# Strassen's scheme for the gate and value products of a fused attention, experts and gated layer, with their weights narrowed ahead of time and kept in DRAM

## The chip, the cores and the metric

The kernel runs on one core of a Trainium2 chip. The metric is the device time of one execution in microseconds; it is compared by the median of several runs. A profile of one execution comes with it: the "span" is the time from its first to its last instruction, and the execution's own time is a little longer.

The engines are named as in the profile: PE (TensorE, matmuls), PEld (its weight loads), DVE (VectorE), ACT (ScalarE), POOL (GpSimd) and SP (SyncE, which issues the DMAs). SBUF is the working memory of 128 partitions, PSUM the memory into which PE writes its sums.

## The reference

Three layers are computed in a row, in float32 and close to its precision:

```python
# attention: q, k, v are [2, 8, 1152, 64]; q is averaged over pairs of rows
q_pool = q.reshape(B, H, S // 2, 2, D).mean(axis=3)
attn = softmax(q_pool @ k.T / sqrt(D));  x = attn @ v      # x: 1152 tokens (2 batches x 576) x 512
# four experts, all of them for every token, weighted by p
for e in range(4):
    out += p[:, e:e+1] * (np.maximum(x @ w1[e], 0) @ w2[e])   # w1 [4,512,1024], w2 [4,1024,512]
# gated layer: w_gate, w_val [512,1536] and w_out [1536,512] come as float64
g = x @ w_gate
return (g * sigmoid(g) * (x @ w_val)) @ w_out                 # [1152, 512]
```

## The kernel before

Every matrix product is made from float32 split in two: a high half `hi` in the reduced format fp32r and the rest `lo = x - hi`. A product is then three matmuls, hi*hi, hi*lo and lo*hi (`gemm`, L918). ACT makes the high half with a copy, DVE (or POOL) the low half with a subtraction.

The token dimension has two batches of 576 tokens. Attention of the first batch runs alone; attention of the second runs together with the first batch's experts; then the second batch's experts run alone on PE; then the gated layer follows for all 1152 tokens. Nothing before the second batch's experts is touched by the change.

*Experts.* Each expert has 8 hidden groups (512 inputs, 128 outputs) and 4 output groups. A weight "piece" is 128 partitions x 512 elements; it is loaded by SP into one of three buffers `wraw`, split by `split_hi` (L350, ACT) and `split_lo` (L357, DVE) into `whi` and `wlo` (two buffers each), and used by 24 matmuls of 288 columns (`products`). A group's sums lie in a pair of PSUM banks, `p0` or `p1` in turn (`expert_bank`); `evict_h` and `evict_h2` (L974, L978) take a hidden group out, `evict_y` (L994, DVE) and `add_y` (L1000, POOL) an output group, into `yacc`.

*Gated layer* (`gated`, L1119). The results `yacc` of both batches are split into `yhi` and `ylo` (L1131, L1132). For each of 12 column chunks, first the gate's and then the value's weights are loaded as 64-bit words (`w64`), narrowed to float32 on DVE (`narrow`, L320: five instructions on L326, L329, L331 and L333), split, and multiplied with the tokens in three stretches of 384: 12 matmuls each, 864 in all. ACT and DVE make silu (L1160, L1161), DVE multiplies by the value (L1167), ACT and POOL split the product for the next layer (L1168, L1169). The output products follow, 324 matmuls of 512 columns: five token tiles together for each weight tile, then the others one by one.

*What sets the order.* `Plan` takes every step with a due time, a cost and what it reads, writes and holds; `arrange` orders the steps by a list schedule over them, and each engine executes its instructions strictly in that order. Attention and the first batch's experts are ordered so; the second batch's experts are only sorted by due time, and `gated` stands in the order in which it is written. Both of these are outside the planner's manual schedule: there the framework's own scheduler may still move instructions.

## Time and profile before

| | |
|---|---|
| median of 3 runs | 912.93 us (912.82 to 914.72) |
| the profiled execution | 913.23 us, of which the span is 911.5 us |
| PE, share of the span | 97% |
| DVE, ACT, POOL | 65%, 51%, 43% |
| DMA | 72.31 MB, mean 79 GB/s |

PE works nearly all the time, so the other shares matter only where they hold PE up. A matmul's duration in the trace is longer than the distance between two matmul starts, since they overlap; the distance is what a matmul costs. The stages that the change touches are the last three: the second batch's experts, the gate and value products, and the output products. The rows further down give their edges.

### The profile page before, as it was taken

What the parts mean: (1) busy time and instruction counts of PE and PEld (TensorE: products, weight loads), DVE (VectorE), ACT (ScalarE), POOL (GpSimd) and SP (SyncE); (2) the same over time, 40 slices, a digit from 0 to 9 for tenths busy, and PEclk for the clock granted to TensorE, in tenths of its full rate; (3) what the DMA queues carried; (4) which work ended last, traced back from release to release, by engine and by line L of the source; (5) the groups of instructions that cost most, each with busy time, mean ns of one, the idle gap of its engine ahead of it and who ended that gap; (6) DMA issues with size and microseconds to landing.
All of it is one profiled execution on the core that took longest, in us unless ns stands there. A gap on an engine that the chain in (4) does not pass through costs nothing.

```text
span 911.5 us, 14995 instructions
## 1 busy us (share of the span) xinstructions
PE 886.3 (97%) x5916; PEld 843.7 (93%) x5916; DVE 590.0 (65%) x895; ACT 463.9 (51%) x790; POOL 388.3 (43%) x266
## 2 busy tenths in 40 slices
PE   6998999999999999999999999999999999999998
PEld 5777778889999999999999999999999999999886
DVE  5778888797666576766855334333478988888700
ACT  5878777877776667766653232232322333333110
POOL 3476555866676885785570000202023333222000
PEclk9999999999999999999999999999999999999999
DMA  5022112313322331212125332323233222323210
GB/s 142 23 68 74 42 52 63 89 62 86 92 66 62 96 104 52 61 55 64 47 72 162 92 95 82 94 81 101 83 97 104 93 87 76 93 90 96 70 70 35
DMA packets 122102, 72.31 MB, mean 79 GB/s; under 512 B 32304, under 2 KB 117296, under 8 KB 122032
## 3 DMA queue, kind: packets, MB, share of 16 engines
q1 hardware_dynamic: 122032, 71.36, 26.8%
q8 instruction: 46, 0.75, 0.3%
q14 instruction: 24, 0.20, 0.1%
HBM read 68.96 MB, written 2.38 MB: 78 GB/s over the span
## 4 chain that ended last, share of the span: by engine, by line
PE 87%; DVE 6%; ACT 3%; issue 2%; POOL 1%; DMA 0%; SPq 0%; DVEq 0%; POOLq 0%; ACTq 0%
PE ps L918 41%; PE g L918 16%; PE av L645 12%; PE o L918 8%; PE sc L538 4%; PE sc L539 3%; DVE acc L567 1%; ACT s L556 1%; PE mt L573 1%; PE tr L482 1%; DVE wlo L357 1%; PE tr L508 1%; ACT kt L498 1%; PE m L595 1%; DVE kt L500 1%
## 5 line engine op out<-in xcount | busy, mean ns | idle before, releaser
L612 POOL TENSOR_TENSOR s<-s,m 128x864 f32<-128x864 f32 x64 | 132.1, 2084 | 71.2 <-ACT m L605 67.9
L350 ACT ACTIVATE whi<-wraw 128x512 fp32r<-128x512 f32 x128 | 80.5, 629 | 155.4 <-PE ps L918 149.4
L918 PE MATMUL ps<-xhi,whi 128*128 128x288 f32 x512 | 152.5, 298 | 1.3 <-DVE hlo L978 1.3
L918 PE MATMUL ps<-hhi,whi 128*128 128x288 f32 x512 | 152.3, 297 | 0.0
L918 PE MATMUL ps<-hhi,wlo 128*128 128x288 f32 x512 | 151.1, 295 | 0.0
L918 PE MATMUL ps<-xhi,wlo 128*128 128x288 f32 x512 | 151.0, 295 | 0.0
L918 PE MATMUL ps<-xlo,whi 128*128 128x288 f32 x512 | 151.0, 295 | 0.0
L918 PE MATMUL ps<-hlo,whi 128*128 128x288 f32 x512 | 150.9, 295 | 0.0
L357 DVE TENSOR_TENSOR wlo<-wraw,whi 128x512 fp32r<-128x512 f32 x96 | 84.6, 881 | 92.3 <-ACT whi L350 92.3
L1000 POOL TENSOR_TENSOR yacc<-yacc,yt 128x576 f32<-128x576 f32 x24 | 42.5, 1770 | 189.2 <-DVE yt L994 189.2
L556 ACT ACTIVATE s<-sc 128x576 f32<-128x576 f32 (+1 forms) x160 | 94.3, 601 | 47.8 <-PE sc L539 46.2
L918 PEld LDWEIGHTS ps<-xhi,whi 128*128 128x128 f32 x512 | 96.2, 188 | 1.7 <-issue 1.5
L918 PE MATMUL g<-yhi,wlo 128*128 128x384 f32 x288 | 96.4, 335 | 0.5 <-DVE wlo L357 0.5
L918 PE MATMUL g<-yhi,whi 128*128 128x384 f32 x288 | 96.2, 335 | 0.5 <-ACT yhi L1131 0.5
L918 PEld LDWEIGHTS ps<-xlo,whi 128*128 128x128 f32 x512 | 96.3, 188 | 0.0
L918 PE MATMUL g<-ylo,whi 128*128 128x384 f32 x288 | 96.3, 334 | 0.0
L918 PEld LDWEIGHTS ps<-hlo,whi 128*128 128x128 f32 x512 | 96.3, 188 | 0.0
L918 PEld LDWEIGHTS ps<-hhi,whi 128*128 128x128 f32 x512 | 96.2, 188 | 0.0
L918 PEld LDWEIGHTS ps<-hhi,wlo 128*128 128x128 f32 x512 | 96.2, 188 | 0.0
L918 PEld LDWEIGHTS ps<-xhi,wlo 128*128 128x128 f32 x512 | 96.2, 188 | 0.0
L538 PE MATMUL sc<-qhi,kt 128*128 128x288 f32 x288 | 90.5, 329 | 5.5 <-DVE acc L567 3.6
L618 ACT ACTIVATE s<-s 128x864 f32<-128x864 f32 x96 | 87.9, 921 | 6.1 <-DVE s L612 4.4
(97 smaller groups left out, 1965.9 us busy)
## 6 DMA issues: line engine op xcount, KB each, us to landing
wraw<-in_moe_w_dram SPq DMA_DIRECT2D x128, 256.0 KB, 2.7
w<-in_moe_w_gate_dram SPq DMA_DIRECT2D x12, 512.0 KB, 3.6
w<-in_moe_w_val_dram SPq DMA_DIRECT2D x12, 512.0 KB, 3.6
w<-in_moe_w_out_dram SPq DMA_DIRECT2D x12, 512.0 KB, 3.5
qraw<-in_q_dram SPq DMA_DIRECT2D x32, 144.0 KB, 2.3
kraw<-in_k_dram SPq DMA_DIRECT2D x14, 288.0 KB, 4.0
v<-in_v_dram SPq DMA_DIRECT2D x8, 288.0 KB, 4.0
vraw<-in_v_dram SPq DMA_DIRECT2D x8, 288.0 KB, 3.0
```

What stands on the lines that cost most here:

```text
L350: nc.scalar.activation(out=hi, in_=t, func=AF.Copy)
L357: eng.tensor_tensor(out=lo, in0=t, in1=hi.bitcast(F32), op=ALU.subtract)
L482: nc.tensor.matmul(pt[:, m * P : (m + 1) * P], kr[:, c].rearrange("p h d -> p (h d)"), ident, is_transpose=True,)
L498: nc.scalar.activation(out=kt[me, sl], in_=pt[me, : 3 * P], func=AF.Copy)
L538: nc.tensor.matmul(ps, wt, qhi, start=True, stop=False)
L539: nc.tensor.matmul(ps, wt, qlo, start=False, stop=True)
L556: nc.scalar.activation(out=s[:, c : c + n, :], in_=ps[:, :n, :W], func=AF.Copy)
L612: eng.tensor_tensor(out=sg, in0=sg, in1=m.unsqueeze(1).to_broadcast([P, 3, W]), op=ALU.subtract)
L618: nc.scalar.activation(out=sg, in_=sg, func=AF.Exp)
L645: nc.tensor.matmul(avs[u][:, :W], w[:, c].rearrange("p t d -> p (t d)"), e, start=(c == 0 and n == 0), stop=(c == KC - 1 and n == len(term ...
L918: nc.tensor.matmul(ps, w, x, start=first and n == 0, stop=last and n == len(terms) - 1)
L1000: nc.gpsimd.tensor_tensor(out=y, in0=y, in1=yts[o], op=ALU.add)
```

## The change

*Products.* Strassen's scheme (Winograd's form) is applied to the gate and value products. Tokens are halved by batch, the 512 inputs into two halves of 256, and the weights' columns into two chunks of 128. A group `n` is two chunks of the gate (n even) or of the value weights (n odd), 12 groups in all. Instead of eight block products a group has seven (`PRODUCTS`, `ORDER`), each of 12 matmuls of 288 columns into a pair of PSUM banks (`product`), 84 products named P0 to P83. Their token operands are blocks of `yacc` or sums of them: `B11`, `B21`, `B22`, and `T1` to `T4`, made in place (`sum_tokens`) and split (`operand_hi`, `operand_lo`).

*Sums.* The four quarters of a group's result come from the seven sums: ACT copies four of them out (`copy_sum`), DVE adds (`add_sum`, four a group, each with one input in PSUM), POOL adds (`add_temp`, three a group). Then ACT's tanh, and DVE's `gate` or `value` in place in SBUF.

*Weights.* All 24 tiles of gate and value weights and 8 of 12 of the output weights are loaded and narrowed during the second batch's experts (`due_wide`: ACT makes the upper part, DVE clamps, shifts and joins). POOL makes the scheme's sums of the weight blocks (`sum_weights`, four a group). SP writes blocks and sums of a group to DRAM (`store_weights`, 512 KB and 384 KB) and reads them back when the products need them (`load_weights`); they are split only then.

*Order.* The second batch's experts and the whole gated layer now go through one `Plan` with `arrange`. The second batch's experts use four bank pairs in turn instead of two. The output products take eight token tiles together for each weight tile, and the ninth at the end; the split of the gated results (`hidden_hi`, `hidden_lo`) moves there, and that of the last token tile is made apart (`end_hi`, `end_lo`).

The tables that set the order: `NARROW`, `OPERAND_DUE`, `SUM_DUE` and others hold due times of these steps; `STEPS` and `BANKS` set the order of the first 21 products and their banks by hand.

```diff
+LATER_SPLIT = (-1.55, -1.29)
+NARROW = (2.48, 10.9, -7.66)
+NARROW_DUE = (0.68, 0.1, 0.2, 4.7, 0.4)
+WEIGHT_DUE = (14.1, 10.6, 10.7, 10.8, 11.5, 11.6)
...
+OUT_FIRST = 8
...
         self.room = room
-        self.psum = ("sc", "av", "m")
-        self.shared = ("v", "vh", "vl")
+        self.psum = ("sc", "av", "m", "G")
+
+        self.shared = ("v", "vh", "vl", "ready")
...
-    def narrow(i, words):
-
-        _, a, b = words.shape
-        words = words.rearrange("p a b -> p (a b)").bitcast(I32)
...
         def expert_bank(group):
-            return "p1" if len(group) == 3 else f"p{(group[0] * (FC1 + MC) + group[1]) % 2}"
+            if len(group) == 3:
+                return "p1"
+            return f"p{(group[0] * (FC1 + MC) + group[1]) % (4 if b else 2)}"
...
+    def load_wide(j):
+        if j < NPIECE:
+            src = columns((wg, wv)[j // 2 % 2], 0, MC, j // 4 * 2 + j % 2)
+        else:
+            c = j - NPIECE
+            src = wo[c * P : (c + 1) * P, :].unsqueeze(1)
+        wides[j] = pools["late"].tile([P, *src.shape[1:]], I64, tag="w64", name=f"w64_{j}", bufs=2)
+        nc.sync.dma_start(out=wides[j], in_=src)
...
+    def take_high(j):
+
+        ups[j] = pools["late"].tile(list(wides[j].shape), F32, tag="up", name=f"up{j}", bufs=1)
+        nc.scalar.activation(out=ups[j], in_=words(j, 1).bitcast(F32), func=AF.Copy, scale=DOWN)
+
+    def clamp(j):
+        nc.vector.tensor_scalar(ups[j], ups[j], LIMIT, -LIMIT, op0=ALU.min, op1=ALU.max)
...
+    def take_low(j):
...
+            n = j // 2
+            bits[n] = pools["st"].tile([P, 2, MC, P], I32, tag="wk", name=f"wk{n}", bufs=3)
+        nc.vector.tensor_scalar(narrowed(j), words(j, 0), 29, None, op0=ALU.logical_shift_right)
+
+    def join(j, m):
+        amount, op = ((3, ALU.logical_shift_left), (SIGN, ALU.bitwise_and))[m]
+        out = narrowed(j)
+        nc.vector.scalar_tensor_tensor(
+            out=out, in0=ups[j].bitcast(I32), scalar=amount, in1=out, op0=op, op1=ALU.bitwise_or
+        )
+
...
+    def sum_weights(n, m):
+
+        if m == 0:
+            wsums[n] = pools["st"].tile([P, 3, 2, P], F32, tag="ws", name=f"ws{n}", bufs=2)
+        s2, s3, s4 = (wsums[n][:, x] for x in range(3))
+        a11, a12, a21, a22 = (weights(n, r, k) for r in range(2) for k in range(2))
+        out, a, b, op = (
+            (s3, a11, a21, ALU.subtract),
+            (a21, a21, a22, ALU.add),
+            (s2, a21, a11, ALU.subtract),
+            (s4, a12, s2, ALU.subtract),
+        )[m]
+        nc.gpsimd.tensor_tensor(out=out, in0=a, in1=b, op=op)
...
+    def store_weights(n, m):
+        if m:
+            nc.sync.dma_start(out=wd[n, :, 4:7], in_=wsums[n])
+        else:
+            nc.sync.dma_start(
+                out=wd[n, :, 0:4].rearrange("p (a k) b c -> p a (k b) c", a=2),
+                in_=bits[n].bitcast(F32),
+            )
+
...
+    PRODUCTS = {
+        1: (0, "B11"), 2: (1, "B21"), 5: (2, "T1"), 4: (3, "T4"),
+        6: (4, "T2"), 7: (5, "T3"), 3: (6, "B22"),
+    }
+    ORDER = (1, 2, 5, 6, 7, 3, 4)
+    STEPS = [(n, p) for n in range(NP) for p in ORDER]
+    STEPS[:21] = (
+        [(n, p) for n in range(2) for p in ORDER[:3]] + [(2, 1), (2, 2), (0, 6), (0, 7), (0, 3)]
+        + [(1, 6), (1, 7), (0, 4), (1, 3), (1, 4)] + [(2, p) for p in ORDER[2:]]
+    )
...
+    def weight_hi(n, g):
+        if g < 3:
+            t = pools["gw"].tile([P, 2, 2, 2, P], F32R, tag="wq", name=f"wq{n}_{g}", bufs=7)
+        else:
+            t = wp.tile([P, 1, 2, 2, P], F32R, tag=single_home(n), name=f"wq{n}_{g}", bufs=2)
+        wsplits[n, g] = t
+        nc.scalar.activation(out=t[:, :, 0], in_=weight_part(n, g), func=AF.Copy)
+
+    def weight_lo(n, g):
+        t = wsplits[n, g]
+        nc.vector.tensor_tensor(
+            out=t[:, :, 1], in0=weight_part(n, g), in1=t[:, :, 0].bitcast(F32), op=ALU.subtract
+        )
+
+    SOURCE = {
+        "B11": (0, 0), "B21": (0, 2), "B22": (1, 2),
+        "T1": (0, 0), "T2": (0, 0), "T3": (1, 0), "T4": (0, 2),
+    }
+    TERMS = {
+        "T1": ((1, 0), (0, 0)), "T2": ((1, 2), (0, 0)),
+        "T3": ((1, 2), (1, 0)), "T4": ((0, 2), (0, 0)),
+    }
...
+    def sum_tokens(name, c):
+        (b0, o0), (b1, o1) = TERMS[name]
+        nc.vector.tensor_tensor(
+            out=source(name, c), in0=yaccs[b0][:, o0 + c, :], in1=yaccs[b1][:, o1 + c, :],
+            op=ALU.subtract,
+        )
...
+    BANKS = (0, 1, 2, 0, 1, 3, 0, 1, 0, 1, 2, 0, 1, 2, 3, 0, 1, 2, 3, 0, 1)
...
+    def product(i, s):
+        if i not in sums:
+            sums[i] = pair(sum_bank(i), f"P{i}")
+        quarter = PRODUCTS[STEPS[i][1]][0]
+        w = wsplits[STEPS[i][0], quarter // 2][:, quarter % 2]
+        t = operands[PRODUCTS[STEPS[i][1]][1]]
+        gemm(
+            sums[i][:, s, :W],
+            [
+                (w[:, x, c], t[:, y, c, subs[s]])
+                for c in range(2)
+                for x, y in ((0, 0), (0, 1), (1, 0))
+            ],
+        )
...
+    def copy_sum(n, i, to):
+        nc.scalar.activation(out=place(n, to), in_=sums[i][:, :, :W], func=AF.Copy)
+
+    def add_sum(n, i, to, other):
+        nc.vector.tensor_tensor(
+            out=place(n, to), in0=sums[i][:, :, :W], in1=place(n, other), op=ALU.add
+        )
+
+    def add_temp(n, to, other):
+        t = place(n, to)
+        nc.gpsimd.tensor_tensor(out=t, in0=t, in1=place(n, other), op=ALU.add)
...
+    def gate(n, q):
+        t = place(n, q)
+        nc.vector.scalar_tensor_tensor(
+            out=t, in0=tanhs.pop((n, q)), scalar=1.0, in1=t, op0=ALU.add, op1=ALU.mult
+        )
...
+        def due_wide(j, t):
+            d = NARROW_DUE
+            at(
+                t + NARROW[2] if j < NPIECE + OUT_FIRST else t - 9, "SP", 0.6, load_wide, j,
+                writes=[("w64", j)], takes=[("w64", ("w64", j))],
+            )
...
+            at(
+                t + d[2], "DVE", 0.7, take_low, j,
+                reads=[("w64", j)] + ([] if opens else [("bits", j - 1)]),
+                writes=[("bits", j)],
+                takes=[("ok" if first else "wraw" if c >= 0 else "wk", tile[0])] if opens else [],
+                uses=[] if opens else tile,
+            )
+            for m in range(2):
+                at(
+                    t + d[3 + m], "DVE", 0.7, join, j, m, kind="port",
+                    reads=[("up", j)], writes=[("bits", j)], uses=tile,
...
+        for i, (n, p) in enumerate(STEPS):
+            t = t0 + i * SLOT
+            if p == ORDER[0]:
+                due_split_weights(n, t0 + 7 * SLOT * n if n > 2 else t0)
+            quarter, name = PRODUCTS[p]
+            g = quarter // 2
+            for s in range(2):
+                at(
+                    t + s * SLOT / 2, "PE", 6 * PITCH, product, i, s, kind="r",
+                    reads=[("wh", n, g), ("wl", n, g)] + [(x, name, c) for x in ("rh", "rl") for c in range(2)],
+                    writes=[("P", i, s)] + ([] if s else [("P", i, 1)]),
+                    takes=[] if s else [(sum_bank(i), ("PT", i))],
+                    uses=[("QS", n, g), ("PT", i)] + [("OP", name)] * (name in ("B11", "B21")),
+                )
+            t += SLOT
+            d = SUM_DUE
+            if p == 1:
+                due_copy(n, i, "s1", t + d[0])
+            elif p == 2:
+                due_copy(n, i, 0, t + d[1])
+                due_temp(n, 0, "s1", t + d[2])
+                due_result(n, 0, t)
+            elif p == 6:
+                due_add(n, i, "u2", "s1", t + d[3])
+                due_add(n, place_of[n, 5], "u4", "u2", t + d[4])
+            elif p == 7:
+                due_add(n, i, "u3", "u2", t + d[5])
+                due_add(n, i, 3, "u4", t + d[6])
+                due_result(n, 3, t)
+            elif p == 3:
+                due_copy(n, i, 1, t + d[8])
+                due_temp(n, 1, "u4", t + d[9])
+                due_result(n, 1, t)
+            elif p == 4:
+                due_copy(n, i, 2, t + d[10])
+                due_temp(n, 2, "u3", t + d[11])
+                due_result(n, 2, t)
```

PE, at the end of the second batch's experts. Before, the last rows of `ps` are followed by the gate's first sum:

```order
L918 MATMUL ps_7686<-hlo_7489,whi127_7705 128x288
L918 MATMUL ps_7686<-hhi_7487,wlo127_7706 128x288
L918 MATMUL g_7793<-yhi_7773,whi128_7742 128x384
L918 MATMUL g_7793<-ylo_7774,whi128_7742 128x384
L918 MATMUL g_7793<-yhi_7773,wlo128_7743 128x384
L918 MATMUL g_7793<-yhi_7773,whi128_7742 128x384
```

Now twelve-matmul products follow (`wqN_g` are the split weights of group N, part g):

```order
L884 MATMUL ps_8103<-hlo_7908,whi127_8112 128x288
L884 MATMUL ps_8103<-hhi_7899,wlo127_8113 128x288
L884 MATMUL P0_8173<-opB11_5636,wq0_0_7982 128x288 x12
L884 MATMUL P1_8189<-opB21_5652,wq0_0_7982 128x288 x12
L884 MATMUL P2_8214<-opT1_8048,wq0_1_7995 128x288 x12
L884 MATMUL P3_8235<-opB11_5636,wq1_0_7936 128x288 x12
L884 MATMUL P4_8253<-opB21_5652,wq1_0_7936 128x288 x12
L884 MATMUL P5_8273<-opT1_8048,wq1_1_7990 128x288 x12
L884 MATMUL P6_8292<-opB11_5636,wq2_0_8145 128x288 x12
L884 MATMUL P7_8311<-opB21_5652,wq2_0_8145 128x288 x12
L884 MATMUL P8_8327<-opT2_8154,wq0_2_8067 128x288 x12
L884 MATMUL P9_8343<-opT3_8271,wq0_2_8067 128x288 x12
```

The first eight products need B11, B21 and T1 alone, of groups 0, 1 and 2; T2 is first used by P8 and T3 by P9.

DVE, in the hidden groups of one of the second batch's experts. Before, weight halves and evictions alternate:

```order
L357 TENSOR_TENSOR wlo98_6729<-wraw98_6639,whi98_6728 128x512
L978 SCALAR_TENSOR_TENSOR hlo_6704<-ps_6674,hhi_6702 128x576
L357 TENSOR_TENSOR wlo99_6766<-wraw99_6672,whi99_6765 128x512
L978 SCALAR_TENSOR_TENSOR hlo_6741<-ps_6709,hhi_6737 128x576
L357 TENSOR_TENSOR wlo100_6801<-wraw100_6707,whi100_6800 128x512
L978 SCALAR_TENSOR_TENSOR hlo_6776<-ps_6746,hhi_6774 128x576
L357 TENSOR_TENSOR wlo101_6836<-wraw101_6744,whi101_6835 128x512
L978 SCALAR_TENSOR_TENSOR hlo_6811<-ps_6781,hhi_6809 128x576
```

Now the narrowing of wide tiles 10 and 11 (`up`, `wk5`) stands between them:

```order
L942 SCALAR_TENSOR_TENSOR hlo_6337<-ps_6272,hhi_6326 128x576
L1115 TENSOR_SCALAR up10_6332<-up10_6332 128x512
L1130 TENSOR_SCALAR wk5_6357<-w64_10_6276 128x512
L1135 SCALAR_TENSOR_TENSOR wk5_6357<-up10_6332,wk5_6357 128x512
L338 TENSOR_TENSOR wlo83_6363<-wraw83_6260,whi83_6362 128x512
L942 SCALAR_TENSOR_TENSOR hlo_6384<-ps_6309,hhi_6372 128x576
L1135 SCALAR_TENSOR_TENSOR wk5_6357<-up10_6332,wk5_6357 128x512
L1130 TENSOR_SCALAR wk5_6357<-w64_11_6321 128x512
L338 TENSOR_TENSOR wlo84_6401<-wraw84_6300,whi84_6400 128x512
L942 SCALAR_TENSOR_TENSOR hlo_6424<-ps_6353,hhi_6411 128x576
L1115 TENSOR_SCALAR up11_6419<-up11_6419 128x512
L1135 SCALAR_TENSOR_TENSOR wk5_6357<-up11_6419,wk5_6357 128x512 x2
```

Between two weight halves two or three narrowing instructions stand, some of which wait for ACT's `up` or for the wide load.

DVE, in the middle of the gate stage. Before, a stretch of the loop over column chunks (`bits` and `up` are the narrowing, `th` and `g` the results):

```order
L357 TENSOR_TENSOR wlo137_8322<-bits137_8317,whi137_8321 128x512
L331 TENSOR_SCALAR bits140_8505<-w64_140_8325 128x512
L333 SCALAR_TENSOR_TENSOR bits140_8505<-up140_8502,bits140_8505 128x512
L1161 SCALAR_TENSOR_TENSOR th_8327<-th_8327,g_8301 128x384
L333 SCALAR_TENSOR_TENSOR bits140_8505<-up140_8502,bits140_8505 128x512
L326 TENSOR_SCALAR up141_8568<-w64_141_8386 128x512
L329 TENSOR_SCALAR up141_8568<-up141_8568 128x512
L1161 SCALAR_TENSOR_TENSOR th_8343<-th_8343,g_8330 128x384
L357 TENSOR_TENSOR wlo138_8383<-bits138_8378,whi138_8382 128x512
L1161 SCALAR_TENSOR_TENSOR th_8359<-th_8359,g_8346 128x384
```

Now one group's sums, with the next group's weight halves (`wq7`) and the gates among them (`s1`, `u4` are the temporaries, `sil3` the gate's results):

```order
L1303 TENSOR_TENSOR s1_6_8968<-P45_9014,s1_6_8968 128x576
L1208 TENSOR_TENSOR wq7_0_9047<-wr7_0_8995,wq7_0_9047 128x2x256
L1208 TENSOR_TENSOR wq7_1_9056<-wr7_0_8995,wq7_1_9056 128x2x256
L1303 TENSOR_TENSOR u4_6_9077<-P44_8997,s1_6_8968 128x576
L1303 TENSOR_TENSOR s1_6_8968<-P46_9030,s1_6_8968 128x576
L1303 TENSOR_TENSOR sil3_9005<-P46_9030,u4_6_9077 128x576
L1208 TENSOR_TENSOR wq7_2_9066<-wr7_1_9021,wq7_2_9066 128x2x256
L1208 TENSOR_TENSOR wq7_3_9085<-wr7_1_9021,wq7_3_9085 128x256
L1317 SCALAR_TENSOR_TENSOR sil3_9005<-th6_3_9106,sil3_9005 128x576
L1317 SCALAR_TENSOR_TENSOR sil3_9005<-th6_1_9115,sil3_9005 128x576
L1317 SCALAR_TENSOR_TENSOR sil3_9005<-th6_2_9155,sil3_9005 128x576
L1324 TENSOR_TENSOR g6_9136<-g6_9136,sil3_9005 128x576
```

The narrowing has gone from this stage, and sums of PSUM with a temporary have come; `s1_6` is the operand of POOL's additions as well.

## Rows read from the trace of the kernel before

**Rows 1.** The page's parts 1 and 2: share and instructions, then tenths by slice.

```profile
span 911.5 us, 14995 instructions
...
PE 886.3 (97%) x5916; PEld 843.7 (93%) x5916; DVE 590.0 (65%) x895; ACT 463.9 (51%) x790; POOL 388.3 (43%) x266
...
PEclk9999999999999999999999999999999999999999
```

**Rows 2.** The chain that ended last: start us, us, engine, what.

```profile
472.98 197.18 PE ps L918 x1488
...
685.44 3.35 POOL yacc L1000
...
834.23 73.49 PE o L918 x324
```

**Rows 3.** PE's timeline at the stage edges: start us, us, engine, what.

```profile
479.18 0.29 PE L918 MATMUL ps<-xhi,whi 128*128 128x288 f32 x1
...
682.70 0.33 PE L918 MATMUL g<-yhi,whi 128*128 128x384 f32 x1
...
834.07 0.39 PE L918 MATMUL o<-whi,gh 128*128 128x512 f32 x1
...
907.33 0.39 PE L918 MATMUL o<-oh,gl 128*128 128x512 f32 x1
```

**Rows 4.** Stretches: us, busy PE, PEld, DVE, ACT, POOL, clock, DMA share, GB/s.

```profile
479.20:682.70 203.50, 203.50 (x1539) 203.50 (x1537) 88.34 (x130) 60.08 (x100) 21.46 (x12) 1.00 0.33 98
...
691.00:834.20 143.20, 143.20 (x828) 143.20 (x827) 122.96 (x215) 48.22 (x94) 43.22 (x35) 1.00 0.28 89
```

**Rows 5.** DVE's timeline in the gate stage.

```profile
690.21 0.69 DVE L333 SCALAR_TENSOR_TENSOR bits<-up,bits 128x512 int32<-128x512 int32 x1
...
690.81 0.55 DVE L1161 SCALAR_TENSOR_TENSOR th<-th,g 128x384 f32<-128x384 f32 x1
...
692.20 1.42 DVE L333 SCALAR_TENSOR_TENSOR bits<-up,bits 128x512 int32<-128x512 int32 x2
...
694.11 0.43 DVE L329 TENSOR_SCALAR up<-up 128x512 f32<-128x512 f32 x1
...
696.45 0.42 DVE L331 TENSOR_SCALAR bits<-w 128x512 int32<-128x512 int32 x1
...
697.52 0.55 DVE L1167 TENSOR_TENSOR g<-th,g 128x384 f32<-128x384 f32 x1
...
697.98 1.04 DVE L333 SCALAR_TENSOR_TENSOR bits<-up,bits 128x512 int32<-128x512 int32 x1
```

**Rows 6.** Groups in the second batch's experts: total us, mean ns, idle before.

```profile
L357 DVE TENSOR_TENSOR wlo<-wraw,whi 128x512 fp32r<-128x512 f32 x63 | 43.4, 689 | 85.4 <-ACT whi L350 85.4
...
L978 DVE SCALAR_TENSOR_TENSOR hlo<-ps,hhi 128x576 fp32r<-128x576 f32 x32 | 24.0, 751 | 0.0
...
L1132 DVE TENSOR_TENSOR ylo<-yacc,yhi 128x576 fp32r<-128x576 f32 x4 | 3.0, 755 | 2.0 <-ACT yhi L1131 2.0
...
L350 ACT ACTIVATE whi<-wraw 128x512 fp32r<-128x512 f32 x63 | 39.7, 631 | 133.4 <-PE ps L918 133.4
```

**Rows 7.** POOL's timeline, in three stretches.

```profile
466.15 1.30 POOL L357 TENSOR_TENSOR wlo<-wraw,whi 128x512 fp32r<-128x512 f32 x1
...
473.29 1.44 POOL L1000 TENSOR_TENSOR yacc<-yacc,yt 128x576 f32<-128x576 f32 x1
...
697.23 1.25 POOL L1169 TENSOR_TENSOR gl<-g,gh 128x384 fp32r<-128x384 f32 x1 [8.44 <-ACT gh L1168]
...
710.22 1.01 POOL L1169 TENSOR_TENSOR gl<-g,gh 128x384 fp32r<-128x384 f32 x1 [0.23 <-ACT gh L1168]
```

**Rows 8.** Two dense stretches, and the weight loads' issues (KB, us to landing).

```profile
5.00:10.00 5.00, 3.19 (x15) 2.93 (x16) 1.57 (x3) 2.30 (x5) 0.44 (x1) 1.00 0.90 215
...
478.00:483.00 5.00, 5.00 (x40) 5.00 (x39) 4.97 (x7) 1.31 (x3) 1.81 (x1) 1.00 0.96 294
...
wraw<-in_moe_w_dram SPq DMA_DIRECT2D x128, 256.0 KB, 2.7
```

More of the change, by code (lines that the diff above doesn't have):

```diff
@@ L920, in gemm @@
             )
-    def three(n, whi, wlo, xhi, xlo):
-        return [
-            (a(c), x(c)) for c in range(n) for a, x in ((whi, xhi), (whi, xlo), (wlo, xhi))
-        ]
     yaccs = {}
@@ L1095, in experts @@
                     if e:
+                        last = b and e == NE - 1 and o >= MC // 2
                         at(
-                            due(n - 1) + 0.7, "POOL", 1.45, add_y, o, kind="port",
+                            due(n - 1) + 0.7, "DVE" if last else "POOL", 0.76 if last else 1.45,
+                            add_y, o, nc.vector if last else nc.gpsimd, kind="port",
                             reads=[y], writes=[("y", b, o)],
@@ new lines, in tile_kernel @@
+    pools = {}
+    wides, ups, bits, wsums, wraws, wsplits, operands = ({} for _ in range(7))
+    sums, temps, sils, tanhs, gs, ghs, wos, ends, outs, ots = ({} for _ in range(10))
+    NPIECE = 2 * FC2
+    NP = FC2
+    TT = NT // P
+    wd = dram.tile([NP, P, 7, 2, P], F32, tag="wd", name="wd")
+    od = dram.tile([OUT_FIRST, P, DM], F32, tag="od", name="od")
+    def load_wide(j):
[6 more added lines that the diff above has]
+        nc.sync.dma_start(out=wides[j], in_=src)
@@ new lines, in gate, with value, hidden_home, hidden_hi @@
+    def gate(n, q):
[3 more added lines that the diff above has]
+        )
+    def value(n, q):
+        t = place(n, q)
+        eng = nc.gpsimd if n == NP - 1 else nc.vector
+        eng.tensor_tensor(out=t, in0=t, in1=place(n - 1, q), op=ALU.mult)
+    def hidden_home(c):
+        return ("acc", "B11", "B21", "acc")[c % 4]
+    def hidden_hi(c):
+        tag = hidden_home(c)
+        pool = acc if tag == "acc" else pools["bz"]
+        ghs[c] = pool.tile([P, 2, NT], F32R, tag=tag, name=f"gh{c}")
+        nc.scalar.activation(out=ghs[c][:, 0], in_=gs[c], func=AF.Copy)
@@ new lines, in out_bank, with out_sum, out_product @@
+    def out_bank(t):
+        return f"p{t // 2 % 4}"
+    def out_sum(t):
+        if t // 2 not in outs:
+            outs[t // 2] = pair(out_bank(t), f"out{t // 2}")
+        return outs[t // 2][:, t % 2]
+    def out_product(c, t):
+        hi, lo = wos[c]
+        if t < TT - 1:
+            gh, gl = (ghs[c][:, x, t * P : (t + 1) * P] for x in range(2))
+        else:
+            gh, gl = (ends[0][:, c, x] for x in range(2))
+        gemm(out_sum(t), [(gh, hi), (gh, lo), (gl, hi)], c == 0, c == FC2 - 1)
```

561 lines of the change are left out of this document (405 added, 156 removed).

## The prediction, made before the result was known

> **What bounds the kernel now.** I read the page's busy shares first, then the chain that ended last, then PE's timeline at the stage edges, and the other engines last. TensorE (PE) is busy 97% of the span at the upper of its two clocks, 2.4 GHz: 9 tenths or more were granted in every slice [rows 1]. The chain ends in three blocks of matmuls with one detour between the first two: 1488 expert matmuls without a gap, a hop over a 3.35 us GpSimd (POOL) addition, the gate and value products, the output products [rows 2]. So time is what PE has to do from the second batch's experts on, and little else. The edges give the price of each stage [rows 3]. The second batch's experts run from 479.18 to 682.70: 203.52 us for 1536 matmuls of 288 columns, 0.1325 us each. The gate and value products run to 834.07: 151.37 us for 864 matmuls of 384 columns, handover included. The output products: 323 steps to 907.33, 0.2268 us each.
> Beside PE the experts leave room: in 203.5 us VectorE (DVE) is busy 88, ACT 60, POOL 21. In the gate stage DVE is busy 123 of 143.2 [rows 4]. The change moves work from the second place to the first.
>
> **The change part by part.**
> *Products.* 864 matmuls go (151.37 us). In their place stand 12 groups of 7 products of 12 matmuls, 1008 of 288 columns, the experts' shape and kind: 1008 x 0.1325 = 133.56 us. That is 17.81 us less. Seven eighths of 151.37 would be 132.4: the shorter matmul pays more per column and gives 1.1 us back.
> *Output and end.* The same 324 matmuls, 324 x 0.2268 = 73.48 us, in another order (eight token tiles for each weight tile, the ninth at the end). From the last matmul's end (907.33 + 0.23) to the span's end 3.94 us remain for a copy and a store [rows 1, 3]; I keep them.
> *Sum.* Attention, the first batch and the second batch's expert matmuls keep their order, so 682.70 stands: 682.70 + 133.56 + 73.48 + 3.94 = 893.68 us of span. The profiled execution took 913.23 us for its span of 911.5, so 1.73 us lie around it: 895.4 us if PE never waits. (Its own time stands 0.3 us above the median of 912.93.) What follows is what PE may wait for.
> *Narrowing beside the experts.* 32 tiles of 128x512 (24 of gate and value weights, 8 of output weights) are narrowed there: on DVE a clamp and a shift of 0.43 and 0.42 and two joins that take 1.42 together [rows 5], 2.27 us a tile, 73 us in all; on ACT one copy each, at 0.63 like the weight copy [rows 6], 20 us. DVE had 63 weight halves of 0.689, 32 evictions of 0.751 and 16 more of a like size [rows 6]: 79.5 us. With four halves of B11 and B21 (0.755) the sum is 156 of 203.5 us, and ACT 80. POOL gains 48 sums of 128x256, which the trace does not show: 384 elements take 1.01 and 512 take 1.30 [rows 7], so about 0.7, with 0 and 1.30 as ends; 34 us, and ten additions to yacc of 1.44 [rows 7]. PE waits if a weight half is late. A piece lasts 24 x 0.1325 = 3.18 us; its successor's buffer comes free as it starts, ACT takes 0.63 and DVE 0.69, so 1.8 us of slack stand against a DVE queue that now always has a join or a shift in front (0.7, or 1.04 when POOL holds it up [rows 5]). Four accumulator pairs instead of two let an eviction end two groups, 6.4 us, later than before. I take 1.0 us of waiting; the ends are 0 and 12 (the rival below).
> *The weights' way through DRAM.* In the experts' 203.5 us the queue moves 61 x 256 KB (expert weights), 32 x 512 (wide weights), 12 x 896 out, 8 x 256 out, 4 x 288 and 1920 KB back: 49.0 MB, 241 GB/s, where the trace has 98 [rows 4]. The densest stretches ran 294 GB/s at a busy share of 0.96, and 215 at 0.90 with the small rows of q and k [rows 8]: 167 to 205 us of transfer. At the first the transfers fit with a fifth to spare, and I take that, since these are rows of 512 B and more. A weight load lands in 2.7 us alone [rows 8]; with a wide load and a store of 512 and 384 KB ahead, 1408 KB / 294 = 4.9 us more, it lands in 7.6, and three buffers give it 9.5. SP issues in order, so a store that waits for POOL holds the next weight load too; the 1.9 us that remain are its cover.
> *The handover.* The old stage's own wait for the last expert columns is in the 151.37 and goes with it. Late next: T2 and T3 need the last expert columns. The new order puts eight products (B11, B21, T1 of three groups) ahead of T2, 8 x 1.59 = 12.7 us, and T3 is read 14.3 us in. DVE has 14 instructions of 0.755 to do by then (two columns of experts, the token sums, their halves), 10.6 us, with two POOL additions of 1.44 in between: 13.5 against 14.3. The cover is thin for the first 21 products; I take 1.2 us, between 0 and 4.
> *Evictions in the gate stage.* Per group (11.13 us of PE): DVE four sums from PSUM (0.751), four gates or values (0.755, by ylo, two inputs in SBUF and 576 elements [rows 6]), 3.5 weight halves (0.689), 8.5 us; ACT four copies, two tanh on average, 3.5 halves, 9.5 instructions at about 0.63, 6.0; POOL three additions of 1.44 [rows 7], 4.3. Each engine fits alone. A sum bank is wanted again four products later, 3.2 us after the sums that read it can start; 0.4 us of waiting over the rest, 0 to 3. So 895.4 + 1.0 + 1.2 + 0.4 = 898.0 us.
>
> **The port, weighed.** DVE's instructions with both inputs in SBUF stretch when POOL works: a join of 0.69 took 1.04 beside POOL's 1.25 at 697.23, while a product with one input in PSUM took its usual 0.55 there [rows 5, 7]. The two do not run side by side, then. The Trainium skill (SBUF — State Buffer, Who interferes with whom) says it as a rule: a DVE instruction with two SBUF inputs and a GpSimd one that reads SBUF exclude each other, and the loser waits for the whole instruction. The trace agrees: 0.35 us more for that join. The rule speaks against this change, which gives POOL more to do beside a fuller DVE; what it would make of the time is rival (3).
>
> **Rivals.**
> (1) No wait at all: 895.4. For it: PE had no gap in 203 us of experts. Against: DVE's spare time was 115 us there and is 48 now.
> (2) The experts starve. Each of the 12 weight sets brings two stores and two wide loads; if each costs PE 1 us, by a late weight half or load, 12 us: 898.0 + 11 = 909. For: 241 of 294 GB/s, one in-order queue. Against: 9.5 us of buffers, four banks.
> (3) The port decides the gate stage, and the change loses. Of each group's 11.13 us DVE has 2.6 spare; POOL wants 4.3. If all of it stops DVE, a group takes 12.8, 12 x 1.67 = 20.0 us: 895.4 + 20.0 + 1.0 = 916.4, slower than before. It costs from 2.6 us of blocking a group on, and cancels the gain at 4.1 of 4.3. Against: four of the twelve DVE instructions read PSUM and are not held, and a DVE instruction starts 0.09 us before the one ahead of it ends (690.21 + 0.69 against 690.81 [rows 5]), 1.0 us more spare a group.
>
> **How the numbers follow.** The forecast, 898.0 with 896 to 902 of its own, gets 0.62; rival (1) 0.13; rival (2), spread over 902 to 912, 0.19; rival (3) 0.06. A change under 0.2% (1.8 us, 911.1 to 914.8) cannot be told from none here: 0.02 of (2) falls there. Faster 0.92, same 0.02, slower 0.06. The range, 894.5 to 908.0, takes in (1) and most of (2), and leaves out (3) and the end of (2).
>
> **What would show it.** PE's 1008 products spaced 0.1325 us; the first one at about 682.7 to 684; idle of PE before expert matmuls under 2 us in total, with wlo or hlo as the releaser; the handover's waits on T2, T3 or on sums, none over 2 us; DVE busy near 160 of the experts' 203 us; transfers at a busy share of 0.7 to 0.85 there. The prediction is wrong if expert matmuls wait for weight loads or wlo again and again, if DVE is busy all through the gate stage with its two-input instructions stretched beside POOL, or if the clock falls below 2.4 GHz after such waits.

## The result, and the profile after

The changed kernel takes 898.5 us (median of 4 runs, 897.19 to 901.6) against 912.88 for the kernel before in the same comparison: a ratio of 0.9843, 95% interval 0.9815 to 0.9872, or 14.4 us less. The forecast was 898.0. The profiled execution took 898.72 us, and its parts are what the rest of this text compares.

The page of the changed kernel, busy time and granted clock:

```profile
span 896.9 us, 15607 instructions
PE 872.0 (97%) x6060; PEld 827.7 (92%) x6060; DVE 672.7 (75%) x943; ACT 522.0 (58%) x880; POOL 445.3 (50%) x316
PEclk9999999999999999999999999999999999999999
```

PE has 97% as before [rows 1], and a shorter span: it still bounds the kernel. The chain that ended last, from the second batch's experts on (start us, us, engine, what):

```profile
472.77 90.99 PE ps L884 x686
...
563.78 1.86 DVE wlo L338
565.68 6.38 PE ps L884 x46
572.44 6.63 PE ps L884 x48
579.08 104.94 PE ps L884 x790
684.02 14.39 PE P L884 x108
698.50 0.77 DVE s L1303
699.29 0.77 DVE u L1303
700.11 118.41 PE P L884 x888
818.52 74.57 PE out L884 x324
```

Before, this stretch was three blocks with one detour at the handover [rows 2]. Now the expert block is cut three times (565.68, 572.44, 579.08), the products once (700.11), and the outputs not at all. The hop over POOL's addition at the handover is gone. PE's timeline gives the edges that answer to [rows 3]:

```profile
478.97 0.29 PE L884 MATMUL ps<-xhi,whi 128*128 128x288 f32 x1
...
683.86 0.29 PE L884 MATMUL P<-opB,wq 128*128 128x288 f32 x1
...
818.36 0.40 PE L884 MATMUL out<-ohi,gh 128*128 128x512 f32 x1
...
892.69 0.39 PE L884 MATMUL out<-ohi,end 128*128 128x512 f32 x1
```

The three stages took 204.89, 134.50 and 74.33 us (the last from first to last matmul start); before they took 203.52, 151.37 and 73.25. The products alone give 16.87 us; experts and outputs give 2.45 back.

The stretches of the experts and of the products (busy PE, PEld, DVE, ACT, POOL, then clock, DMA share, GB/s):

```profile
479.20:684.00 204.80, 204.38 (x1538) 203.56 (x1537) 172.57 (x258) 84.49 (x142) 61.59 (x59) 1.00 0.75 239
...
702.00:818.50 116.50, 116.50 (x877) 116.50 (x877) 103.79 (x130) 60.26 (x103) 51.55 (x33) 1.00 0.26 81
```

Against [rows 4] DVE's work in the experts has doubled (88 to 172.6 us) and the traffic has gone from 98 to 239 GB/s; PE lost 1.37 us by it.

The first of the three cuts, in the timeline of ACT, POOL, DVE and PE:

```profile
559.11 0.67 ACT L1112 ACTIVATE up<-w 128x512 f32<-128x512 f32 x1 [2.58 <-DMA w<-in_moe_w_val_dram]
...
562.54 0.69 ACT L1112 ACTIVATE up<-w 128x512 f32<-128x512 f32 x1 [2.24 <-DVE wk L1135]
...
563.12 0.62 ACT L332 ACTIVATE whi<-wraw 128x512 fp32r<-128x512 f32 x1
563.66 1.43 POOL L964 TENSOR_TENSOR yacc<-yacc,yt 128x576 f32<-128x576 f32 x1 [4.55 <-DVE yt L958]
...
563.78 1.85 DVE L338 TENSOR_TENSOR wlo<-wraw,whi 128x512 fp32r<-128x512 f32 x1 [0.27 <-ACT whi L332]
...
565.68 0.40 PE L884 MATMUL ps<-hhi,wlo 128*128 128x288 f32 x1 [0.28 <-DVE wlo L338]
```

Read it upwards from PE. It waits for a weight half on DVE that took 1.85 us instead of 0.69, beside POOL's addition; that half could only start at 563.78, since ACT's copy stood behind the upper part of a wide weight; and that one had waited for joins of an earlier tile whose load ACT had waited 2.58 us for. (A "join" is one of the two DVE instructions that put the upper and the lower part of a wide weight together.) Two causes offer themselves: the port that DVE and POOL share, and the late load.

Mean distance between matmul starts (ns) in each of the twelve output steps of 24 matmuls (the 36 matmuls of the ninth token tile, which follow, take 226.7 in the changed kernel), worked out from PE's starts, in the changed kernel and in three of the experiments below:

```
step          0     1     2     3     4     5     6     7     8     9    10    11
changed   227.4 234.2 234.2 226.8 226.8 234.2 234.2 226.8 226.8 234.2 234.2 226.9
pad32     229.0 233.3 233.2 227.9 226.6 233.3 233.2 227.9 226.6 233.3 233.3 227.9
home      234.0 228.3 249.8 234.2 234.2 226.9 226.7 234.2 234.2 226.8 226.8 233.9
pad352    227.7 226.7 226.7 226.7 226.7 226.7 226.6 226.7 226.7 226.7 226.7 226.7
```

Six steps of the changed kernel cost 234.2 ns a matmul where five cost 226.8 and the first 227.4. They are those whose hidden operand lies where B11 and B21 lay.

### The profile page after: what moved, and what is told of

Read it like the earlier page. It is cut to its first block, busy times and chain, and to the rows that moved or that the text cites. A ratio compares the mean times of both kernels' runs of the same rounds, so it can differ in the third digit from the quotient of the medians.

```text
span 896.9 us, 15607 instructions
## 1 busy us (share of the span) xinstructions
PE 872.0 (97%) x6060; PEld 827.7 (92%) x6060; DVE 672.7 (75%) x943; ACT 522.0 (58%) x880; POOL 445.3 (50%) x316
## 4 chain that ended last, share of the span: by engine, by line
PE 88%; DVE 6%; ACT 3%; issue 1%; POOL 1%; DMA 0%; SPq 0%; DVEq 0%; ACTq 0%; POOLq 0%
PE ps L884 43%; PE P L884 15%; PE av L611 12%; PE out L884 8%; PE sc L504 4%; PE sc L505 3%; DVE acc L533 1%; ACT s L522 1%; PE mt L539 1%; PE tr L448 1%; DVE wlo L338 1%; ACT kt L464 1%; DVE kt L466 1%; PE tr L474 1%; PE m L561 1%
## 5 line engine op out<-in xcount | busy, mean ns | idle before, releaser
L338 DVE TENSOR_TENSOR wlo<-wraw,whi 128x512 fp32r<-128x512 f32 x96 | 90.4, 941 | 22.4 <-ACT whi L332 21.9
L505 PE MATMUL sc<-qlo,kt 128*128 128x288 f32 x288 | 81.2, 297 | 0.0
L596 POOL TENSOR_TENSOR el<-s,eh 128x864 fp32r<-128x864 f32 x32 | 68.4, 2142 | 25.9 <-ACT eh L589 18.7
L884 PE MATMUL P<-opT,wq 128*128 128x288 f32 x576 | 80.6, 295 | 0.0
L611 PE MATMUL av<-s,v 128*128 128x288 f32 x288 | 77.3, 409 | 0.8 <-ACT s L584 0.8
```

Of the source, the lines that this page charges most:

```text
L338: eng.tensor_tensor(out=lo, in0=t, in1=hi.bitcast(F32), op=ALU.subtract)
L505: nc.tensor.matmul(ps, wt, qlo, start=False, stop=True)
L596: eng.tensor_tensor(out=lo, in0=src, in1=parts[u, g][0].bitcast(F32), op=ALU.subtract)
L611: nc.tensor.matmul(avs[u][:, :W], w[:, c].rearrange("p t d -> p (t d)"), e, start=(c == 0 and n == 0), stop=(c == KC - 1 and n == len(term ...
L884: nc.tensor.matmul(ps, w, x, start=first and n == 0, stop=last and n == len(terms) - 1)
```

## The experiments

Twelve kernels, each the changed one with one edit (up2 and early have pad352's as well). "Experts", "products" and "outputs" are the three lengths as above; in the changed kernel 204.89, 134.50 and 74.33 us.

**What an eighth product costs (eight).**

```diff
-        gemm(sums[i][:, s, :W], ...)
+        for _ in range(2 if STEPS[i][1] == 4 else 1):
+            gemm(sums[i][:, s, :W], ...)
```

> Each group's last product is computed twice into the same bank pair (the second time in place of the first), so that PE does eight block products a group instead of seven and all else stays. Theory (PE bound): 12 products of 12 matmuls of 0.133 us come on top, 19.2 us: 917.5 to 917.9, slower than the kernel of before; the saved eighth is the whole gain. Rival (sums bound): if PE already waits hidden in the pace of the sums, part of the 19.2 us is absorbed, and the time stays under 915.

Measured: 918.19 us (916.75 to 919.71), 1.0054 of before (1.0034 to 1.0074). PE's edges:

```profile
683.53 0.29 PE L884 MATMUL P<-opB,wq 128*128 128x288 f32 x1
...
837.20 0.40 PE L884 MATMUL out<-ohi,gh 128*128 128x512 f32 x1
```

The products took 153.67 us, 19.17 more for 144 matmuls, 0.1331 each: PE's own price, with nothing absorbed. The saved eighth is more than the whole gain; with eight products the change loses 5 us.

**POOL's additions of the experts on DVE (add_dve).**

```diff
-                        last = b and e == NE - 1 and o >= MC // 2
+                        last = b
```

> In the second batch the ten additions to yacc that POOL did are done by DVE. Theory (port): the three waits of the experts (565.11, 572.02 and 578.78 us; 1.37 us with the slow matmul after each) come from weight halves on DVE that stretch to 1.85 and 1.78 us beside POOL's addition of 1.4 to 1.8 us. With the additions on DVE at 0.76 no weight half is held so long: the experts fall from 204.89 to 203.5 to 203.8 us, the time to 897.2. Rival (full queue): DVE is simply too full with the narrowing; with 7.6 us more on it the waits stay or grow, 204.9 to 207 us, 898.5 to 900.5.

Measured: 899.07 us (898.78 to 900.02); experts 205.01, with waits of 0.50 and 0.62 us at 571.63 and 594.65. DVE and ACT ahead of the first:

```profile
569.80 0.68 ACT L1112 ACTIVATE up<-w 128x512 f32<-128x512 f32 x1 [3.92 <-DMA w<-in_moe_w_gate_dram]
570.39 0.62 ACT L332 ACTIVATE whi<-wraw 128x512 fp32r<-128x512 f32 x1
570.52 0.43 DVE L1115 TENSOR_SCALAR up<-up 128x512 f32<-128x512 f32 x1 [0.29 <-ACT up L1112]
...
571.53 0.68 DVE L338 TENSOR_TENSOR wlo<-wraw,whi 128x512 fp32r<-128x512 f32 x1
```

The weight half takes its usual 0.68 us, and PE waits all the same, because ACT waited 3.92 us for a wide load. So the port is not the cause of this wait. In two of the changed kernel's three cuts it had its part: their weight halves ran beside POOL's addition, the first as shown above, the other here:

```profile
577.25 1.78 DVE L338 TENSOR_TENSOR wlo<-wraw,whi 128x512 fp32r<-128x512 f32 x1 [0.28 <-ACT whi L332]
```

At 0.69 us they would have ended at 564.47 and 577.94 (an estimate), before PE came to need them at 565.24 and 578.91. There the wait takes both, an ACT copy that is late and POOL's addition. The full-queue rival fits the size, but not the rows at 570.

**A byte, a join, a buffer, an earlier load (store2, no_join, up2, early).** Cut to the lines that matter:

```diff
+        for to in (wd2, wd):            # store2: each weight store twice
...
     def join(j, m):                     # no_join
+        if m == 0 or j >= 0:            # always true
+            return
...
-        ... tag="up", ..., bufs=1)      # up2
+        ... tag="up", ..., bufs=2)
...
-NARROW = (2.48, 10.9, -7.66)            # early
+NARROW = (2.48, 10.9, -9.5)
```

> Each of the 24 weight stores to DRAM is made twice (the first copy into a second array that nobody reads): 10.75 MB more during the experts, 49 to 60 MB or 291 GB/s in 204.9 us. Theory (late loads: the experts' waits begin with a wide weight load that lands late, ACT's copy of its upper part stands ahead of the expert weight's copy in ACT's order, and the weight half follows late): more bytes make more wide loads late, and the waits grow from 0 to 1.4 us to 4 to 15 us: 901 to 912. Rival (DVE and POOL alone make the waits): DMA has room left, the experts stay at 203.5 to 205 us, the time at 897 to 899.

Measured: 909.69 us (908.11 to 910.03), ratio 0.9955 (0.9939 to 0.997); experts 216.37 us. The experts, and five microseconds after the longest wait:

```profile
478.90:695.20 216.30, 208.23 (x1537) 206.24 (x1536) 171.31 (x258) 84.64 (x142) 60.72 (x59) 0.98 0.83 277
582.00:587.00 5.00, 5.00 (x22) 5.00 (x23) 3.59 (x4) 0.71 (x1) 2.10 (x2) 0.51 0.77 270
```

With 10.75 MB more and DVE as busy as before (171.3), PE lost 12.9 us. Part of it is the clock: after a wait of 2.9 us at 577.53 the granted clock was 0.51, its lower level (1.2 GHz), and the matmuls came 0.24 us apart until 586.9, which cost some 2.5 us (an estimate: 23 matmuls from 580.2 to 586.8, 0.11 us each). The longest waits follow late wide loads, as the theory says: ACT waited 3.6 to 7.8 us for four of them between 535 and 580. They were late in two ways: the one that ACT could use at 579.31 was issued 3.6 us after the weight load ahead of it (1.6 for the same one in the changed kernel), since two more stores stand before it in SP's order, and a wide load took 6.3 to 7.1 us to land in the median (5.7 to 6.3). The run does not part the bytes from the issues.

> The 64 joins of the narrowing are left out (the narrowed weights are then wrong in value, and the output with them), 49 us less on DVE during the experts. Theory (DVE's queue): the waits come from weight halves that stand behind a full DVE; without the joins none is left: experts 203.5 us. Rival (late loads): ACT's copy still waits for wide loads that land late, and with it the expert weight's copy behind it; the waits stay, 0.3 to 1.4 us in those executions that have them.

Measured: 897.27 and 897.29 us; experts 203.51, no wait in the profiled execution. ACT still waited 2.89 us for a wide load, and the expert weight's copy stood right behind:

```profile
568.46 0.68 ACT L1112 ACTIVATE up<-w 128x512 f32<-128x512 f32 x1 [2.89 <-DMA w<-in_moe_w_gate_dram]
569.04 0.62 ACT L332 ACTIVATE whi<-wraw 128x512 fp32r<-128x512 f32 x1
...
570.18 0.68 DVE L338 TENSOR_TENSOR wlo<-wraw,whi 128x512 fp32r<-128x512 f32 x1
```

It was not late enough to hold PE up: in the changed kernel ACT could use the same load at 569.98. The run with swapped products (below) has all the joins and almost the same three starts (568.42, 568.98, 570.14), and no wait there either. So this run does not show that the joins are needed for a wait. What parts all thirteen profiled executions is when ACT starts on that tile, counted from the experts' first matmul: up to 89.9 us (early, pad32, no_join, swap) the experts lose 0 to 0.24 us, from 90.4 us on (the nine others; 91.01 in the changed kernel) 0.75 us or more.

> As with 352 bytes at the top of SBUF, and the upper parts of the narrowing (up) alternate between two buffers; each engine's order of instructions stays. Theory (in-order chain: a wide load that lands some 2 us later than in other executions makes ACT's copy of one upper part late, DVE's joins of it end late, the next upper part waits for its one buffer, and the expert weight's copy stands behind it on ACT): with two buffers the second link is gone, and the waits fall from 1.4 to 1.8 us to at most 0.6: experts 203.5 to 204.1 us, time 895.2 to 896.0 against 896.4. Rival (DVE's queue): the weight halves stand behind the joins on DVE anyway; the waits stay at 1.4 to 1.8 us, 896.1 to 897.4.

Measured: 896.95 us (896.05 to 898.84); experts 204.30. The wait at 565 is gone, and so are those at 579, where the second link stood; the one at 571.7 (0.80 us with the slow matmul) is left:

```profile
570.10 0.67 ACT L1112 ACTIVATE up<-w 128x512 f32<-128x512 f32 x1 [4.16 <-DMA w<-in_moe_w_gate_dram]
570.67 0.62 ACT L332 ACTIVATE whi<-wraw 128x512 fp32r<-128x512 f32 x1
...
571.81 0.68 DVE L338 TENSOR_TENSOR wlo<-wraw,whi 128x512 fp32r<-128x512 f32 x1
...
572.54 0.40 PE L884 MATMUL ps<-hhi,wlo 128*128 128x288 f32 x1 [0.52 <-DVE wlo L338]
```

A second buffer cannot help there: the load itself was late. The missing wait at 565 is no proof of the second link, since home, add_dve and pool3 have one buffer and no wait there either. The time does not tell it from pad352's.

> As with 352 bytes at the top of SBUF, and the wide loads are due 1.84 us earlier (SP issues some of them one or two places further ahead). Theory (late loads): they land in time, ACT does not wait for them at 556 to 570 us, and the experts take 203.5 us, the time 895.0 to 895.6. Rival (two buffers): the load then waits on SP for its buffer, and holds the expert weights' loads and the stores behind it; the waits move and stay at 1 to 3 us: 896 to 898.

Measured: 897.48 us (896.28 to 898.58); experts 203.52, no wait. The loads were in time, as the theory says. The time is not what it gave, for two other reasons that the trace shows: attention, which the edit does not touch, took 1.6 us longer in the profiled execution, and the products took 135.17, with a new wait of 0.9 us at 727.39 for a copy of a sum on ACT (the plan's order of the products moved with the due times). The first is the clock, which fell to its lower level in attention: 9 matmuls where pad352 (second row) has 17.

```profile
77.40:80.60 3.20, 3.20 (x9) 2.21 (x9) 1.91 (x4) 2.16 (x3) 1.58 (x2) 0.50 0.77 236
77.40:80.60 3.20, 3.20 (x17) 2.52 (x16) 2.06 (x4) 3.15 (x6) 1.45 (x2) 1.00 0.77 245
```

Of the four executions two had a mean granted clock of 0.998 (898.46, the profiled one, and 898.58) and two of 1.0 (896.28 and 896.5). In the 7 us before 77 PE was busy 5.90 us (5.75 in pad352, where the clock stayed at its upper level, 2.4 GHz), so why it fell stays open, and so does whether this version is faster than pad352.

**Where a weight operand lies (pad32, home, pad352).**

```diff
-for name, stack in (("late", ctx), ...
+for name, stack in (("pad", ctx), ("late", ctx), ...
+pools["pad"].tile([P, 8], F32, ...)     # pad32; 88 in pad352
...
-return ("acc", "B11", "B21", "acc")[c % 4]   # home
+return ("B11", "acc", "acc", "B21")[c % 4]
```

> A tile of 32 bytes is put at the top of SBUF, so that everything on the right side (the operands B11 and B21, the hidden operands in their places, the split weights wq, the gated results) starts 32 bytes lower, at a multiple of 64 bytes instead of 32 beyond one. Theory (address): the output steps whose hidden operand lies at 32 beyond a multiple of 64 (weight tiles 1, 2, 5, 6, 9, 10) cost 0.2342 us a matmul instead of 0.2268 because of that address. Then all steps come to 0.2267, the output stage falls from 74.33 to 73.3 us, and the products, whose weights move too, from 0.1334 towards 0.1325 a matmul (up to 0.5 us): 897.0 to 897.4 instead of 898.5. Rival (neighbours): those six steps are slow because ACT and DVE split the next hidden tile beside them, or because of their place in the loop; then the stage stays at 74.3 and the time at 898.5.

Measured: 898.15 us (896.73 to 898.24). The products' pace fell from 133.0 to 132.6 ns a matmul (0.47 us of the stage, 134.03), nearly as expected; the outputs stayed at 74.31, with six steps at 233.3 ns. For the outputs the theory as put (a multiple of 64 bytes suffices) is wrong. Experts 203.51: this execution had no wait. Its ACT rows beside those shown above:

```profile
557.19 0.68 ACT L1112 ACTIVATE up<-w 128x512 f32<-128x512 f32 x1 [0.70 <-DMA w<-in_moe_w_val_dram]
...
561.01 0.68 ACT L1112 ACTIVATE up<-w 128x512 f32<-128x512 f32 x1 [1.83 <-DVE wk L1135]
```

The same load, waited for 0.70 us instead of 2.58: the order of instructions is the same in both, and their times first part at a wide load issued at 542, which ACT could use at 546.02 here and at 547.04 there.

> The hidden operands of the output products change places: tiles 0, 3, 4, 7, 8 and 11 go where B11 and B21 lay, the others to the two tiles that come free on the left. Theory (the tile's address decides, within 512 bytes or by side): the slow steps of 0.2342 us a matmul become 0, 3, 4, 7, 8 and 11; the stage stays within 0.2 us of 74.33. Rival (place in the loop, or what ACT and DVE do beside it): 1, 2, 5, 6, 9 and 10 stay the slow ones.

Measured: 898.51 us in one run; the slow steps became 0, 3, 4, 7, 8 and 11 (table above; step 2 holds a wait of 0.5 us for DVE's half of an output weight). They follow the tile, not the loop. The stage came to 74.92, 0.59 above the changed kernel's, 0.51 of it that wait.

> The tile at the top of SBUF has 352 bytes, so that the right side starts at 128 beyond a multiple of 512 bytes, as the tiles on the left do (480 beyond one as it was, 448 with 32 bytes, where the six slow output steps still took 0.2333 us a matmul). Theory (place within 512 bytes): hidden operands at the left side's residue cost the same on both sides; all output steps come to 0.2267 to 0.2275, the stage falls from 74.3 to 73.3 us, the products stay at 0.1325 as with 32 bytes: about 895.5 to 897.5. Rival (side): tiles high up in SBUF are slow to load as weights whatever the residue; the six steps stay at 0.233 to 0.234, the stage at 74.3, the time at 898.

Measured: 896.44 us (896.06 to 897.37), ratio 0.9815 (0.9799 to 0.9831). All twelve steps fell to 226.7 ns (227.7 in the first), and the outputs to 73.24:

```profile
818.20 0.39 PE L884 MATMUL out<-ohi,gh 128*128 128x512 f32 x1
...
891.43 0.39 PE L884 MATMUL out<-ohi,end 128*128 128x512 f32 x1
```

The tiles lie as high in SBUF as before but for 352 bytes, so the side is excluded; the start address decides. That 512 bytes are the period is not shown: the two fast places, 0 and 128, are also multiples of 128, and the two slow ones, 448 and 480, are not. Products 134.18 (132.7 ns), experts 205.28: this execution had the late load again, and took 897.37; the other three took 896.06 to 896.63. It is the fastest version with a reason shown for its gain (1.09 us in the outputs, 0.3 in the products). By total time alone its interval overlaps that of the changed kernel.

**The handover (swap).**

```diff
-  ... (0, 6), (0, 7), (0, 3)] + [(1, 6), (1, 7), (0, 4), ...
+  ... (0, 6), (0, 7), (1, 6)] + [(0, 3), (1, 7), (0, 4), ...
-BANKS = (0, 1, 2, 0, 1, 3, 0, 1, 0, 1, 2, 0, 1, ...
+BANKS = (0, 1, 2, 0, 1, 3, 0, 1, 0, 1, 0, 2, 1, ...
```

> The products P10 and P11 change places (group 1's T2 product, into the bank pair p0 that is free by then, ahead of group 0's B22 product into p2). Theory (bank): P10 waited 0.28 us at 699.70 (0.39 with the slow matmul after it) for the bank pair that DVE's second addition gave free at 700.05; a product later that pair has been free for about 1.2 us, and the wait goes: products 134.50 to 134.1 us, time 898.1. Rival (sums): DVE's chain of additions is late as a whole, and the wait moves to P11 to P14, with 0.4 us or more as before.

Measured: 899.35 us (899.13 to 899.75); products 136.62, experts 203.76. PE around the exchange:

```profile
698.55 1.05 PE L884 MATMUL P<-opB,wq 128*128 128x288 f32 x6
...
699.45 1.76 PE L884 MATMUL P<-opT,wq 128*128 128x288 f32 x12
...
701.04 0.96 PE L884 MATMUL P<-opB,wq 128*128 128x288 f32 x6
...
702.74 0.53 PE L884 MATMUL P<-opT,wq 128*128 128x288 f32 x2 [0.74 <-ACT sil L1300]
```

The list schedule put the first half of the B22 product ahead again, so it waited 0.27 us for its bank pair as before, and two new waits of 0.9 us came for copies on ACT. The bank theory was not tested; that a product here waits for its pair's reader is shown only by the changed kernel's row (700.11 begins as DVE's second sum ends at 700.05).

**POOL's share of the port in the products (pool2, pool3).**

```diff
         nc.gpsimd.tensor_tensor(out=t, in0=t, in1=place(n, other), op=ALU.add)
+        nc.gpsimd.tensor_tensor(out=s, in0=t, in1=t, op=ALU.add)   # pool2
+        nc.gpsimd.tensor_tensor(out=s, in0=s, in1=s, op=ALU.add)   # pool3
```

> After each of POOL's additions of the products' sums stands a second one into a tile that nobody reads: 36 more instructions of 1.43 us or more on POOL in the gate and value products, 54 us there become about 106 of 134.5; nothing waits for them but POOL. Theory (port): a DVE instruction with both inputs in SBUF does not run beside POOL's. In the changed kernel these took 19 us longer than alone in this stage (24 gates 1.00 against 0.755, 20 values 1.075, 29 weight halves 0.885 against 0.689), and DVE was busy 103.8 of 116.5 us. Twice the POOL work makes it 38 us, DVE passes the span of the stage, and PE waits 5 to 20 us: 904 to 919. Rival (only POOL's own time counts): the stage stays at 134.5 to 136 us, the time at 897 to 900.

Measured: 924.1 us in one run; products 159.0. The expectation overlooked that the gates and values write in place the tile that the extra instruction reads, and so wait for it (7.8 and 9.5 us of DVE's idle time from 702 to 820). The granted clock was also at its lower level (0.50) in four stretches of over 3 us behind such waits, some 5.6 us of the stage (an estimate from the matmuls' distances there). It cannot tell the two apart; the next can.

> As the run before with a second POOL instruction after each of the 36 additions, but it reads and writes only its own tile, so that no instruction of DVE has to wait for it (before, the gates and values, which write the tile in place, had to wait until it had been read). Theory (port): POOL's busy time in the products is what counts, about 105 us of it against 56; DVE's two-input instructions, 56 to 75 of 119 us busy, stretch further, DVE has no gap left, and PE waits 10 to 25 us: stage 145 to 160 us, time 908 to 924. Rival (dependence): the 924 us came from gates and values that had to wait for the reading; without it the stage takes 134.5 to 137 us, the time 898 to 901.

Measured: 920.02 us (919.87 to 920.55), ratio 1.0078 (1.0055 to 1.0101); products 156.26. The stage, and DVE's and POOL's groups from 702 to 818 us (total us, mean ns, idle before):

```profile
683.40:839.60 156.20, 139.80 (x1010) 136.02 (x1009) 145.97 (x147) 70.69 (x122) 111.89 (x71) 0.99 0.20 62
```

```profile
L1329 DVE TENSOR_TENSOR g<-g,sil 128x576 f32<-128x576 f32 x18 | 30.5, 1721 | 4.0 <-POOL g L1309 4.0
L1322 DVE SCALAR_TENSOR_TENSOR sil<-th,sil 128x576 f32<-128x576 f32 x19 | 23.2, 1243 | 3.2 <-ACT th L1318 2.3
...
L1314 POOL TENSOR_TENSOR spare<-spare 128x576 f32<-128x576 f32 x27 | 41.3, 1529 | 0.0
```

Instructions that no other engine waits for cost 21.8 us: the values took 1.72 us and the gates 1.24, against 0.755 alone, and the sums with an input in PSUM their usual 0.75. DVE was busy 146 of 156.2 us. Two smaller parts are not the port: DVE waited 4.0 us for POOL's own additions, which stand behind the extra ones in POOL's order, and after the waits at 721 and 724 the clock was at its lower level for some 3 us, about 1.4 us of the stage:

```profile
723.90:727.10 3.20, 3.20 (x14) 3.20 (x15) 2.00 (x4) 2.27 (x5) 1.50 (x1) 0.50 0.70 245
```

The Trainium skill (SBUF — State Buffer, Who interferes with whom) has the rule that a DVE instruction with two SBUF inputs and a GpSimd one that reads SBUF exclude each other; the trace agrees: gates and values, which have two, stretched. It is what one join showed before [rows 5, 7]. POOL's 56 us in this stage let PE run on, 112 do not.

## Why the prediction was right, point by point

**The sum.** From 895.4 (no wait) to the profiled 898.72: the experts started 0.21 earlier, lost 1.37 in waits (1.0 forecast), the handover lost 0.39 (1.2), the products' pace cost 0.55 (0, with 0.4 for waits that did not come), the outputs 1.07 (0), and 0.16 lies at the end and around the span. The total of 3.3 against 2.6 is near because errors cancelled.

**The products.** 1008 matmuls were priced at 0.1325 us and cost 0.1330: right in kind, as the eight-product run shows by its own 0.1331. The missing half nanosecond is mostly the operands' address; pad32 gives 0.1326.

**The outputs.** The step that failed is "the same 324 matmuls, 324 x 0.2268". The same shape cost 0.2342 in half of the steps, for the place of the tile that PE loads as weights.

**The experts.** The waits came near the size forecast and with `wlo` as the releaser, but not by the path: the forecast had the weight half stand in DVE's queue, and the runs show the delay begin with a late wide load that ACT's order hands on to the expert weight's copy; the prediction priced no such wait for wide loads. So the 1.0 is in part luck. DMA was right to the megabyte (48.9 MB, 239 GB/s). That it would fit was less sure than the prediction has it: its 167 us are at the 294 GB/s of a row, its 205 at 215 GB/s scaled up to a full busy share; taken alike they are 160 to 205, or 167 to 228, and both upper ends are longer than the stage's 203.5. DVE was mis-sized: 172.6 us busy instead of 156. The weight halves took 0.783 instead of 0.689, the joins 0.77 instead of 0.71, and the clamps, which have one input, 0.605 instead of 0.43. POOL held all three up: the 21 clamps with no POOL instruction beside them took 0.42 on average, the 11 others 0.96. The weight sums on POOL, which the trace of before did not show, took 0.83 to 0.91 us on average where 0.7 was taken.

**The handover.** The 1.2 us stood for T2 and T3 coming late. They came in time; the 0.39 us are a wait of P10 for the bank pair that DVE's second sum gives free (700.05, then 700.11).

**Rival (2), starving experts,** was not met, but is close by: a fifth more bytes, in twice as many stores, brought 909.7 us, by late loads as it named. That this is its own price of 909 is chance, since some 2.5 us of it are the clock. **Rival (3), the port,** decides once POOL's work in the products doubles: 920. Its objection was right: DVE had room for the blocking, 103.8 of 116.5 us busy with it. **Rival (1)** is what pad32, no_join and early show for the experts: 203.5 us with no wait at all.

## What to carry to other kernels

A kernel bound by PE gains what its matmuls cost, if the work that this moves elsewhere fits with all its stretching: count the DVE instructions that POOL holds up (here those with two SBUF inputs, and the clamps) and POOL's of a stage as one queue. An in-order engine that makes the next weights should have no instruction ahead of them that waits for a transfer; no run here moved one away, but early, which issued the transfers sooner, had no wait. When matmuls of one shape cost differently in one program, compare the addresses of their tiles first.
